# Softmax scores scaled and negated in place by the instruction that takes their minimum, the 1e-9 taken from padding columns, and new keys for the order of the work

## The chip, the core and the metric

The kernel runs on one core of a Trainium2 chip. The core's engines work side by side, each through its own queue in order: PE (TensorE, matrix products, with PEld its weight loads), DVE (VectorE), ACT (ScalarE), POOL (GpSimd) and SP (SyncE, which here only issues transfers). Matrix products write to PSUM; PSUM and SBUF are the two on-chip memories. The metric is the time on the device in microseconds (us); before the change it is 1153.44 us, the median of three runs between 1152.08 and 1154.72.

## What is computed

Attention with a threshold on the scores, and a feed-forward layer behind it:

```python
scores = scale * np.matmul(q, k.transpose(0, 1, 3, 2))          # q, k, v: (8, 8, 576, 64), scale = 1/8
thresh = np.max(scores, axis=-1, keepdims=True) - tau
scores = np.where(scores >= thresh, scores, -1000000000.0)
scores = scores - np.max(scores, axis=-1, keepdims=True)
attn = np.exp(scores)
attn = attn / (np.sum(attn, axis=-1, keepdims=True) + 1e-09)
x = np.matmul(attn, v)                                          # then laid out as (4608, 512)
h = x @ w_in                                                    # w_in: (512, 2048)
g = np.where(h >= 1, h, np.where(h <= -1, 0.0, (h + 1) ** 2 / 4))
out = g @ w_out                                                 # w_out: (2048, 512)
```

All of it is in float32 or wider. The kernel forms every product from float16 pairs, a high part and the rest, so each large product is a sum of several float16 products.

## The kernel before, in words

The attention part is cut into 288 score tiles of 128 query rows by 576 keys, for two heads at a time; 36 tiles belong to each of the 8 batches. One tile goes through this chain: `qk` (PE, L840) writes the scores into one of two PSUM buffers `s`; `smax` (DVE, L851 to L853) takes the negated row maximum and makes from it the bias of the exponential and the threshold; `sexp` (ACT, L856) writes the exponential of the scaled scores to SBUF (`e`); `smask` (DVE, L860) multiplies it by "score at or above the threshold" and sums the row; `sden` (DVE, L864 and L865) adds 1e-9 and takes the reciprocal; `snorm` (POOL, L868) multiplies the row; `shi` (ACT, L873) and `slo` (POOL, L876) make the float16 pair `hl`; `send` (SP, L879) transposes it by a transfer into `eT`; `av` (PE, L946) multiplies it with the values. Tiles 0 and 1 take a shorter way with a PE transpose (L912). The buffer `s` is free again when `smask` has read it.

The scale of a pair of heads is a column of the small tile `pc`, made on POOL by `scales3` (L391 to L394, four instructions for each of 32 pairs). It is one number for the exponential's scale and one for the threshold.

The feed-forward part follows by groups of 256 tokens: `ffn1` (PE, L1024) into one of three PSUM buffers `ph`, `relu` and `square` (ACT, L1030 and L1033), `gate` (DVE, L1037, in place in PSUM), the float16 pair by `ghi` (ACT, L1042) and `glo` (DVE, L1047), `ffn2` (PE, L1073) into the only PSUM buffer `acc`, and `evict` (ACT, L1093), which must have read `acc` before the next 128 tokens may begin there. In the first 200 us the weights are also unpacked (`b2`, `b3` on DVE, L660 and L664) and split (L725, L737), and PE fills long gaps with products of ones (`keep_warm`, L1109).

The order of the work on every engine is worked out ahead, in Python: each step is an `Op` with an engine, an assumed cost and a key, and a simulated list scheduler (`Plan.order`) takes, for each engine that falls idle, the ready step with the lowest key. The table `SHIFT` moves single keys. The order that comes out is fixed: each engine's queue on the chip holds the steps in it, and waits where a step's input is late. The assumed costs decide only the order.

Of the kernel before, what the change touches and what calls it, by code (L numbers as in the profile page):

```python
# [22 lines left out]
NPT = 2  # L23
# [26 lines left out]
WARM = (1.0, 200, 0.6, 0.056)  # L50

SHIFT = {
    "bits o": {7: -20, 8: -2, 12: -2},
    "den": {73: 5},
    "ffn": {8: 5, 12: -2, 19: 2, 21: -2, 22: -1.71, 23: -5},
    "ffn2": {1: 10, 9: -5, 10: 5, 16: 5, 18: -7.1, 19: -40, 23: -2, 24: 2, 25: -2, 26: -2},
    "load i": {0: -20, 1: -20, 11: -1.07},
    "load o": {8: 2},
    "load q k": {8: 4.48, 10: -4.1},
    "load v": {8: 19.78, 11: 5},  # L60
    "low o": {0: -19.88, 1: -18.87, 2: -16.6, 3: -10, 4: -10, 5: -5, 6: -5, 8: -2},
    "move": {8: -5, 9: -13.89},
    "norm": {39: -2, 58: -2, 69: -2},
    "parts o": {12: -2},
    "q k": {7: 20, 10: -5},
    "q k parts": {1: -8.79, 8: 5, 10: -5},
    "qk": {87: 25.43},
    "scale o": {0: -20},
    "send": {62: -5, 63: -10},
    "tile": {7: -2, 14: -2, 29: 5, 42: -2, 51: -2, 73: -10},  # L70
    "v": {1: 5, 2: 5},
    "v parts": {7: 17.66, 8: 35.35, 9: 33.43, 11: 11.83},
}
# [19 lines left out]
class Plan:  # L93
# [19 lines left out]

    def op(self, eng, cost, key, fn, after=(), take=(), uses=(), work=0.0, behind=None, mode=0, leave=0):

        o = Op(eng, cost, round(key, 3), fn, work)
        o.n = len(self.ops)
# [12 lines left out]
        return o  # L130
# [97 lines left out]
def attn_ffn_kernel(ctx: ExitStack, tc: tile.TileContext, qT, kT, vT, tau, w_in, w_out, out):  # L228
# [7 lines left out]
    B, H, D, S = qT.shape  # L236
# [8 lines left out]
    SP = -(-S // P) * P  # L245
# [36 lines left out]
    es = ring("e", 4, [SP], F32)  # L282
# [34 lines left out]
    def ap(b, arr):  # L317
        return arr[b.slot]
# [67 lines left out]
    def more_scales(cb, so, key):  # L386
        def scales3():
            c = ap(cb, pc)
            u = c[:, 8:14].rearrange("p (v t) -> p v t", t=2)
            x = c[:, 14:20].rearrange("p (v t) -> p v t", t=2)  # L390
            G.tensor_scalar(c[:, 24:27], u[:, :, 0], 2.0 ** 102 * D ** -0.5, 1.0, ALU.mult, ALU.mult)  # L391
            G.tensor_scalar(c[:, 27:30], x[:, :, 0], tcs[:, 2:3], 1.0, ALU.mult, ALU.mult)
            G.tensor_tensor(c[:, 24:27], c[:, 24:27], u[:, :, 1], ALU.mult)
            G.tensor_tensor(c[:, 27:30], c[:, 27:30], x[:, :, 1], ALU.mult)  # L394

        return plan.op("POOL", 0.85, key - 2, scales3, [so], uses=[cb])

    def add_qk(b, p, need):

# [408 lines left out]


    part_tr = {}  # L810
    eTb = {}
    av_op = {}
    prev = {}

    def chained(name, o):
        prev[name] = o
        return o

    def add_tile(j):
# [19 lines left out]
                        k = ap(kb, kk)[h, 0, kl, f * SH : (f + 1) * SH] if not b else ap(kb, kk)[:, hd, kl, f * SH : (f + 1) * SH]  # L839
                        T.matmul(ap(s, s_ps)[r, f, :SH], q, k, start=ql == kl == 0, stop=kl == 1)  # L840

        def sv():
            return ap(s, s_ps)[:, :, :SH]

        def halves(t):
            return t.rearrange("p (f n) -> p f n", f=2)

        def smax():

            t, c = ap(m, sm), ap(cb, pc)  # L850
            V.tensor_reduce(t[:, 0:1], sv(), AX.XY, ALU.max, negate=True)  # L851
            V.tensor_scalar(t[:, 1:2], t[:, 0:1], c[:, 24 + v : 25 + v], None, ALU.mult)  # L852
            V.tensor_scalar(t[:, 2:3], t[:, 0:1], -1.0, c[:, 27 + v : 28 + v], ALU.mult, ALU.add)  # L853

        def sexp():
            A.activation(halves(ap(e, es)[:, :S]), sv(), AF.Exp, bias=ap(m, sm)[:, 1:2], scale=ap(cb, pc)[:, 24 + v : 25 + v])  # L856

        def smask():
            t = ap(m, sm)
            V.scalar_tensor_tensor(halves(ap(e, es)[:, :S]), sv(), t[:, 2:3], halves(ap(e, es)[:, :S]), ALU.is_ge, ALU.mult, accum_out=t[:, 3:4])  # L860

        def sden():
            t = ap(m, sm)
            V.tensor_scalar(t[:, 4:5], t[:, 3:4], 1e-9, 1.0 / ESC, ALU.add, ALU.mult)  # L864
            V.reciprocal(t[:, 5:6], t[:, 4:5])  # L865

        def snorm():
            G.tensor_scalar(ap(e, es)[:, :S], ap(e, es)[:, :S], ap(m, sm)[:, 5:6], 1.0, ALU.mult, ALU.mult)  # L868

        w = S if b else SP  # L870

        def shi():
            A.activation(ap(x, hl)[:, :S], ap(e, es)[:, :S], AF.Copy)  # L873

        def slo():
            G.tensor_tensor(ap(x, hl)[:, w : w + S], ap(e, es)[:, :S], ap(x, hl)[:, :S], ALU.subtract)  # L876
# [6 lines left out]
        if b and v == 2 and i - 1 in av_op and tiles[first[i] - 1][1] == 2:  # L883
            o.behind.append(av_op[i - 1])
            av_op[i - 1].left += 1
        o = chained("max", plan.op("DVE", 1.03, jt, smax, [o, c2], take=[m], uses=[s, cb], behind=prev.get("max")))
        o = chained("exp", plan.op("ACT", 0.73, jt, sexp, [o], take=[e], uses=[s, m, cb], behind=prev.get("exp")))
        o = plan.op("DVE", 0.76, jt, smask, [o], uses=[s, m, e])
        o = plan.op("DVE", 0.28, plan.key("den", j, j), sden, [o], uses=[m])
        take = [eTb[i]] if j == first[i] else []  # L890
        if j >= NPT:
            o = chained("norm", plan.op("POOL", 0.73, jn, snorm, [o], uses=[e, m], behind=prev.get("norm")))
            o = chained("hi", plan.op("ACT", 0.58, jn, shi, [o], take=[x], uses=[e], behind=prev.get("hi")))
            o = plan.op("POOL", 1.26, jn, slo, [o], uses=[e, x])
            o = chained("tr", plan.op("SP", 1.45, plan.key("send", j, j), send, [o], take=take, uses=[x, eTb[i]], work=1.7, behind=prev.get("tr")))
# [266 lines left out]
```

## Time and profile before

| | before |
|---|---|
| median of 3 runs | 1153.44 us (1152.08 to 1154.72) |
| profiled execution, first to last instruction | 1151.1 us |
| PE busy | 1114.2 us (97%) |
| DVE busy | 949.8 us (83%) |
| ACT busy | 899.7 us (78%) |
| POOL busy | 800.9 us (70%) |
| mean granted TensorE clock | 0.991 |

The profile gives the span of one profiled execution; its own time has no other figure, and the median of the runs lies 2.3 us above that span. A busy share is a mean over the whole span, and the stretches differ: the start, with the weights, is not the middle. A row of a group gives line, engine, operation, what is written and read, the count, then busy time, the mean duration of one, and the idle time just before.

### The profile page before, as it was taken

The numbers are of one execution on the slowest core, as the hardware profiler recorded it, in microseconds if no ns is written. First come the engines' busy times: TensorE is split into PE (matmuls) and PEld (weight loads), VectorE is DVE, ScalarE is ACT, GpSimd is POOL, SyncE is SP. The second block draws the span as 40 slices with busy tenths as digits, with TensorE's granted clock in tenths as the row PEclk, the third lists the DMA queues.
The fourth block names the chain that finished last, engine by engine and source line by source line (L and its number), as shares of the span: only waits on it lengthen the run. The fifth ranks groups of instructions, "written<-read, shape, count | busy, mean of one in ns | idle before, by whom it ended". The sixth has DMA issues, their size and how long they took to land.

```text
span 1151.1 us, 27628 instructions
## 1 busy us (share of the span) xinstructions
PE 1114.2 (97%) x9627; PEld 770.1 (67%) x9627; DVE 949.8 (83%) x2995; ACT 899.7 (78%) x1692; POOL 800.9 (70%) x957
## 2 busy tenths in 40 slices
PE   8789999999999999999999999999999999999998
PEld 6447556767677577676677677676667677676673
DVE  5899987988889988899889989888889889885241
ACT  6989777979788789777887789776888788685362
POOL 4678999688875788668966887758966788654000
PEclk9969999999999999999999999999999999999999
DMA  8788699879895999777986899658876899554000
GB/s 322 289 220 151 124 196 203 165 135 206 163 181 98 187 167 200 148 127 168 202 182 109 154 207 204 121 108 186 182 178 103 157 183 171 103 103 83 19 1 28
DMA packets 435930, 179.41 MB, mean 156 GB/s; under 512 B 400464, under 2 KB 407632, under 8 KB 435792
## 3 DMA queue, kind: packets, MB, share of 16 engines
q1 hardware_dynamic: 435792, 177.67, 75.1%
q8 instruction: 75, 1.23, 0.4%
q14 instruction: 63, 0.52, 0.1%
HBM read 45.09 MB, written 9.44 MB: 47 GB/s over the span
## 4 chain that ended last, share of the span: by engine, by line
PE 63%; DVE 13%; POOL 8%; ACT 5%; issue 4%; DMA 4%; SPq 1%; ACTq 0%; DVEq 0%; POOLq 0%
PE ph L1024 24%; PE acc L1073 23%; PE s L840 8%; PE ph L946 7%; POOL hl L876 3%; DVE sm L851 3%; DVE e L860 3%; DMA eT<-hl 2%; POOL e L868 2%; POOL nat L461 1%; ACT e L856 1%; POOL raw L448 1%; DMA raw<-in_v_dram 1%; ACT hl L873 1%; DVE sm L852 1%
## 5 line engine op out<-in xcount | busy, mean ns | idle before, releaser
L876 POOL TENSOR_TENSOR hl<-e,hl 128x576 f16<-128x576 f32 x286 | 367.5, 1290 | 100.7 <-ACT hl L873 97.5
L1024 PE MATMUL ph<-x,WI 128*128 128x256 f16 (+1 forms) x4032 | 401.6, 257 | 1.1 <-DVE gb L1047 0.7
L1024 PEld LDWEIGHTS <-WI 128*128 128x128 f16 x4032 | 346.5, 98 | 52.9 <-issue 5.0
L868 POOL TENSOR_SCALAR e<-e,sm 128x576 f32<-128x576 f32 x286 | 218.4, 768 | 108.9 <-DVE sm L865 73.2
L856 ACT ACTIVATE e<-s,sm,pc 128x576 f32<-128x576 f32 x288 | 238.1, 832 | 53.3 <-DVE sm L852 37.9
L860 DVE SCALAR_TENSOR_TENSOR e<-s,sm,e 128x576 f32<-128x576 f32 x288 | 231.3, 812 | 30.5 <-ACT e L856 25.5
L873 ACT ACTIVATE hl<-e 128x576 f16<-128x576 f32 x286 | 194.9, 684 | 65.7 <-POOL e L868 53.1
L851 DVE TENSOR_REDUCE sm<-s 128x1 f32<-128x576 f32 x288 | 215.4, 748 | 25.8 <-PE s L840 24.0
L840 PE MATMUL s<-kk,qq 128*128 128x288 f16 (+3 forms) x1360 | 193.5, 290 | 15.1 <-DVE e L860 11.2
L1073 PE MATMUL acc<-WO,ga 128*128 128x512 f16 x864 | 206.5, 379 | 0.8 <-ACT ob L1093 0.8
L840 PEld LDWEIGHTS <-qq 128*128 128x128 f16 (+3 forms) x1360 | 113.3, 100 | 88.9 <-issue 45.3
L1037 DVE SCALAR_TENSOR_TENSOR ph<-ph,fcs,asq 128x512 f32<-128x512 f32 (+1 forms) x160 | 111.9, 700 | 51.8 <-ACT asq L1033 50.8
L1030 ACT ACTIVATE asq<-ph,fcs 128x512 f32<-128x512 f32 (+1 forms) x160 | 116.3, 738 | 48.6 <-PE ph L1024 47.9
L1073 PEld LDWEIGHTS <-ga 128*128 128x128 f16 x864 | 81.5, 98 | 82.7 <-issue 4.5
L946 PE MATMUL ph<-eT,vst 128*64 128x320 f16 (+2 forms) x1928 | 124.1, 280 | 3.7 <-DMA eT<-hl 1.3
L946 PEld LDWEIGHTS <-vst 128*64 128x64 f16 x1928 | 98.7, 110 | 26.7 <-issue 17.5
L1033 ACT ACTIVATE asq<-asq 128x512 f32<-128x512 f32 x144 | 90.9, 631 | 2.1
L1047 DVE SCALAR_TENSOR_TENSOR ga<-ph,fcs,ga 128x256 f16<-128x256 f32 (+1 forms) x160 | 70.6, 450 | 23.0 <-ACT WO L1042 8.8
L1042 ACT ACTIVATE ga<-ph,fcs 128x256 f16<-128x256 f32 (+1 forms) x160 | 70.3, 450 | 23.1 <-DVE ph L1037 20.8
L1073 PE MATMUL acc<-WO,gb 128*128 128x512 f16 x300 | 72.8, 379 | 0.0
L461 POOL TENSOR_TENSOR nat<-raw,nat 128x576 f16<-128x576 f32 x56 | 71.7, 1292 | 1.1 <-ACT nat L454 1.0
L852 DVE TENSOR_SCALAR sm<-sm,pc 128x1 f32<-128x1 f32 x288 | 61.7, 214 | 10.4
(167 smaller groups left out, 1245.8 us busy)
## 6 DMA issues: line engine op xcount, KB each, us to landing
kk<-nat SPq DMA_DIRECT2D x112, 144.0 KB, 2.7
raw<-in_v_dram SPq DMA_DIRECT2D x32, 288.0 KB, 3.9
raw<-in_q_dram SPq DMA_DIRECT2D x32, 288.0 KB, 4.1
raw<-in_k_dram SPq DMA_DIRECT2D x32, 288.0 KB, 3.8
WO<-in_moe_w_in_dram SPq DMA_DIRECT2D x16, 512.0 KB, 8.3
out_dram<-ob SPq DMA_DIRECT2D x32, 256.0 KB, 2.5
qq<-nat SPq DMA_DIRECT2D x112, 72.0 KB, 2.2
x<-in_moe_w_out_dram SPq DMA_DIRECT2D x10, 512.0 KB, 4.3
```

The source lines that it names most:

```text
L840: T.matmul(ap(s, s_ps)[r, f, :SH], q, k, start=ql == kl == 0, stop=kl == 1)
L851: V.tensor_reduce(t[:, 0:1], sv(), AX.XY, ALU.max, negate=True)
L856: A.activation(halves(ap(e, es)[:, :S]), sv(), AF.Exp, bias=ap(m, sm)[:, 1:2], scale=ap(cb, pc)[:, 24 + v : 25 + v])
L860: V.scalar_tensor_tensor(halves(ap(e, es)[:, :S]), sv(), t[:, 2:3], halves(ap(e, es)[:, :S]), ALU.is_ge, ALU.mult, accum_out=t[:, 3:4])
L868: G.tensor_scalar(ap(e, es)[:, :S], ap(e, es)[:, :S], ap(m, sm)[:, 5:6], 1.0, ALU.mult, ALU.mult)
L873: A.activation(ap(x, hl)[:, :S], ap(e, es)[:, :S], AF.Copy)
L876: G.tensor_tensor(ap(x, hl)[:, w : w + S], ap(e, es)[:, :S], ap(x, hl)[:, :S], ALU.subtract)
L946: T.matmul(o[hd * D : (hd + 1) * D, :n], vt[:, k, hd * D : (hd + 1) * D], t[:, kb, hd * n : (hd + 1) * n], start=m == 0, stop=m == len(blo ...
L1024: T.matmul(h[:, i], WTh["i"][:, u, wl * 512 + c * P : wl * 512 + (c + 1) * P], x[:, cc, xl, c0 : c0 + n].rearrange("p (t n) -> p t n", n=P ...
L1030: A.activation(tv()[:, :, c], hv()[:, :, c], AF.Relu, bias=fcs[:, b, q, 2 : 3], scale=fcs[:, b, q, 1 : 2])
L1037: V.scalar_tensor_tensor(hv()[:, :, c], hv()[:, :, c], fcs[:, b, q, 0 : 1], tv()[:, :, c], ALU.max, ALU.min)
L1073: T.matmul(ap(ab, accs), gv(h, gl)[:, x], WTh["o"][:, fc + i, wl * 512 : (wl + 1) * 512], start=fc + i == 0 and m == 0, stop=fc + i == NFC ...
```

## The change

`smax` becomes one `tensor_scalar` that multiplies the scores by a negative scale in place in PSUM and takes their minimum into `sm` by its accumulator. That minimum is the bias of the exponential, whose scale is now the constant -1. A new step `sthr` (DVE) adds tau for the threshold. `smask` compares with "at or below" and runs over one more column in each half, where `e` holds 0.5e-9 and `s` holds -3.0e38; both are written by `pads` (DVE) once for each buffer. So the row sum already holds the 1e-9, and `sden` is a reciprocal alone. `snorm` multiplies by the constant that `sden` had folded in. `scales3` makes one number instead of two, in two instructions. A second way through a tile (`mask_s`, `den_s`, `hi_s`, `lo_s`) is added but chosen for no tile, since `BYSUM` and `HOWS` are empty. The assumed costs of the steps change with this, a table `OFF` adds a constant to the keys of each kind of step, and `SHIFT` grows from 63 to 577 entries. Every matrix product stays as it was, but 188 products of ones are issued instead of 204.

```diff
 SHIFT = {
-    "den": {73: 5},
+    "_evict": {16: -56.49, 17: -0.75},
+    "den": {73: 5, 102: -1.12, 103: 30.8, 208: -2.8, 209: -250.25, 216: 8.96, 217: -8.51, 232: -45.33, 233: -10.82},
...
+OFF = {"av": -2.37, "b2": 28.6, "b3": 134.31, "consts": -11.77, "diff": 34.02, "ends_": -103.45, "evict": 96.25, "f0": -54.27, "f1": 0.14, "f2": 60.57, "f3": 110.84, "f4": 77.96, "f5": 14.45, "f_scale": -9.23, "ffn1": 0.16, "ffn2": 0.17, "fix": 55, "gate": -3.92, "ghi": -1.84, "glo": -1, "gram": 6.16, "hi": 3.9, "largest": -169.25, "lo": 0.04, "load": 0.21, "low": -19.44, "mixed": 325.86, "move": 1.36, "norm": 3.65, "o_scale": 23.37, "qk": -3.81, "relu": -87.18, "rest": -16.41, "rest1": -19.94, "scales": -1.36, "scales2": -6.69, "scales3": -0.38, "sden": -6.48, "send": -2.5, "sexp": 4.71, "shi": -4.76, "slo": -42.44, "smask": -1.99, "smax": 1.28, "snorm": -2.76, "split": -17.76, "split1": -11.94, "square": 0.81, "ssq": 166.71, "sthr": -4.13, "store": -6.38, "sums": 0.23, "tau_consts": 171, "thi": 193.92, "tlo": -9.03, "turn": -326.94, "warm_up": 249.88}
+BYSUM = set()
+HOWS = ""
+EPS = 1e-9
...
+        key = key + OFF.get(name, 0) + SHIFT.get("_" + name, {}).get(i, 0)
...
-        V.tensor_scalar(tcs[:, 2:3], tau_sb, 0.0, -(2.0 ** -102) * D ** 0.5, ALU.max, ALU.mult)
+        V.tensor_scalar(tcs[:, 2:3], tau_sb, 0.0, None, ALU.max)
...
-            x = c[:, 14:20].rearrange("p (v t) -> p v t", t=2)
-            G.tensor_scalar(c[:, 24:27], u[:, :, 0], 2.0 ** 102 * D ** -0.5, 1.0, ALU.mult, ALU.mult)
-            G.tensor_scalar(c[:, 27:30], x[:, :, 0], tcs[:, 2:3], 1.0, ALU.mult, ALU.mult)
+            G.tensor_scalar(c[:, 24:27], u[:, :, 0], -(2.0 ** 102) * D ** -0.5, 1.0, ALU.mult, ALU.mult)
             G.tensor_tensor(c[:, 24:27], c[:, 24:27], u[:, :, 1], ALU.mult)
-            G.tensor_tensor(c[:, 27:30], c[:, 27:30], x[:, :, 1], ALU.mult)
-
-        return plan.op("POOL", 0.85, key - 2, scales3, [so], uses=[cb])
+        return plan.op("POOL", 0.42, key - 2, scales3, [so], uses=[cb])
...
         def smax():
             t, c = ap(m, sm), ap(cb, pc)
-            V.tensor_reduce(t[:, 0:1], sv(), AX.XY, ALU.max, negate=True)
-            V.tensor_scalar(t[:, 1:2], t[:, 0:1], c[:, 24 + v : 25 + v], None, ALU.mult)
-            V.tensor_scalar(t[:, 2:3], t[:, 0:1], -1.0, c[:, 27 + v : 28 + v], ALU.mult, ALU.add)
+            V.tensor_scalar(sv(), sv(), c[:, 24 + v : 25 + v], None, ALU.mult, ALU.min, accum_out=t[:, 0:1])
+
+        def sthr():
+            t = ap(m, sm)
+            V.tensor_scalar(t[:, 2:3], t[:, 0:1], tcs[:, 2:3], None, ALU.add)
 
         def sexp():
-            A.activation(halves(ap(e, es)[:, :S]), sv(), AF.Exp, bias=ap(m, sm)[:, 1:2], scale=ap(cb, pc)[:, 24 + v : 25 + v])
+            A.activation(ev(), sv(), AF.Exp, bias=ap(m, sm)[:, 0:1], scale=-1.0)
+
+        def pads():
+            if e.slot not in padded["e"]:
+                padded["e"].add(e.slot)
+                V.memset(ap(e, es)[:, : 2 * (SH + 1)].rearrange("p (f n) -> p f n", f=2)[:, :, SH:], EPS / 2)
+            if s.slot not in padded["s"]:
+                padded["s"].add(s.slot)
+                V.memset(ap(s, s_ps)[:, :, SH : SH + 1], -3.0e38)
 
         def smask():
             t = ap(m, sm)
-            V.scalar_tensor_tensor(halves(ap(e, es)[:, :S]), sv(), t[:, 2:3], halves(ap(e, es)[:, :S]), ALU.is_ge, ALU.mult, accum_out=t[:, 3:4])
+            if early:
+                padded["s"].discard(s.slot)
+                padded["e"].discard(e.slot)
+                V.scalar_tensor_tensor(ev(), sv(), t[:, 2:3], ev(), ALU.is_le, ALU.mult, accum_out=t[:, 3:4])
+                return
+            pads()
+            V.scalar_tensor_tensor(ev(SH + 1), sv(SH + 1), t[:, 2:3], ev(SH + 1), ALU.is_le, ALU.mult, accum_out=t[:, 3:4])
 
         def sden():
             t = ap(m, sm)
-            V.tensor_scalar(t[:, 4:5], t[:, 3:4], 1e-9, 1.0 / ESC, ALU.add, ALU.mult)
-            V.reciprocal(t[:, 5:6], t[:, 4:5])
+            if early:
+                V.tensor_scalar(t[:, 3:4], t[:, 3:4], EPS, None, ALU.add)
+            V.reciprocal(t[:, 5:6], t[:, 3:4])
 
         def snorm():
-            G.tensor_scalar(ap(e, es)[:, :S], ap(e, es)[:, :S], ap(m, sm)[:, 5:6], 1.0, ALU.mult, ALU.mult)
+            G.tensor_scalar(ev(), ev(), ap(m, sm)[:, 5:6], ESC, ALU.mult, ALU.mult)
...
-        o = chained("max", plan.op("DVE", 1.03, jt, smax, [o, c2], take=[m], uses=[s, cb], behind=prev.get("max")))
-        o = chained("exp", plan.op("ACT", 0.73, jt, sexp, [o], take=[e], uses=[s, m, cb], behind=prev.get("exp")))
-        o = plan.op("DVE", 0.76, jt, smask, [o], uses=[s, m, e])
-        o = plan.op("DVE", 0.28, plan.key("den", j, j), sden, [o], uses=[m])
+        o = chained("max", plan.op("DVE", 0.78, jt, smax, [o, c2], take=[m], uses=[s, cb], behind=prev.get("max")))
+        o2 = plan.op("DVE", 0.18, jt, sthr, [o], uses=[m])
+        o = chained("exp", plan.op("ACT", 0.64, jt, sexp, [o], take=[e], uses=[s, m], behind=prev.get("exp")))
+        jd = plan.key("den", j, j)
...
```

Two places show what the new keys do to the queues. In an order row, a name ends in the buffer's number, and `x2` stands for two such instructions in a row.

The first place is DVE's queue at the start, where tiles 2 and 3 (statistics `sm_124` and `sm_125`, scores `s_61` and `s_62`) come, in the 20 to 75 us of the profile. Before:

```order
L851 TENSOR_REDUCE sm_124<-s_61 128x1
L852 TENSOR_SCALAR sm_124<-sm_124,pc_118 128x1
L853 TENSOR_SCALAR sm_124<-sm_124,pc_118 128x1
L851 TENSOR_REDUCE sm_125<-s_62 128x1
L852 TENSOR_SCALAR sm_125<-sm_125,pc_118 128x1
L853 TENSOR_SCALAR sm_125<-sm_125,pc_118 128x1
```

With the change:

```order
L908 TENSOR_SCALAR s_61,sm_124<-s_61,pc_118 128x2x288
L908 TENSOR_SCALAR s_62,sm_125<-s_62,pc_118 128x2x288
L912 TENSOR_SCALAR sm_124<-sm_124,tcs 128x1
L711 SCALAR_TENSOR_TENSOR WO<-x_106,ph_65 128x512
L912 TENSOR_SCALAR sm_125<-sm_125,tcs 128x1
L921 MEMSET e_93 128x2
L924 MEMSET s_61 128x2
L934 SCALAR_TENSOR_TENSOR e_93,sm_124<-s_61,sm_124,e_93 128x578
L921 MEMSET e_94 128x2
L924 MEMSET s_62 128x2
L934 SCALAR_TENSOR_TENSOR e_94,sm_125<-s_62,sm_125,e_94 128x578
```

Where three instructions of each tile stood, the two large ones now stand next to each other, the threshold of the first tile follows the second tile's minimum, a weight unpacking (L711, L660 before) stands between the two thresholds, and the four `MEMSET` rows are `pads`, which each buffer gets once.

The second place is the end of ACT's queue: the last steps of the feed-forward part, with the evictions of the last two blocks of 128 tokens (`ob`, L1093 before, L1201 now). Before:

```order
L1030 ACTIVATE asq_101<-ph_65,fcs 128x4x64 x2
L1033 ACTIVATE asq_101<-asq_101 128x512
L1042 ACTIVATE ga_111<-ph_65,fcs 128x2x64 x2
L1042 ACTIVATE WO<-ph_65,fcs 128x2x64 x2
L1093 ACTIVATE ob_102<-acc,scs 128x512
L1093 ACTIVATE ob_102<-acc,mix 128x512
```

With the change:

```order
L1150 ACTIVATE ga_110<-ph_64,fcs 128x2x64 x2
L1150 ACTIVATE gb_114<-ph_64,fcs 128x2x64 x2
L1201 ACTIVATE ob_102<-acc,scs 128x512
L1138 ACTIVATE asq_101<-ph_65,fcs 128x4x64 x2
L1141 ACTIVATE asq_101<-asq_101 128x512
L1150 ACTIVATE ga_111<-ph_65,fcs 128x2x64 x2
L1150 ACTIVATE WO<-ph_65,fcs 128x2x64 x2
L1201 ACTIVATE ob_102<-acc,mix 128x512
```

Before, the last two evictions stand together behind the last feed-forward step, and on PE the last 96 products of `ffn2`, 48 for each of the two blocks, follow each other with nothing between. Now the eviction of the block before the last stands ahead of that step, and PE has the step's 48 products of `ffn1` between the two blocks of `ffn2`.

More of the change, by code (lines that the diff above doesn't have):

```diff
@@ L810, in attn_ffn_kernel @@
     part_tr = {}
+    padded = {"e": set(), "s": set()}
     eTb = {}
@@ L894, in add_tile @@
[L894 to L895 removed]
+            ends = []
+            for how in HOWS or ("S" if j in BYSUM else "P"):
+                plan.alt = ("tile", j, how)
+                if how == "S":
+                    n = plan.op("DVE", 0.76, jt, mask_s, [o, o2], uses=[s, m, e])
+                    n = plan.op("DVE", 0.28, jd, den_s, [n], uses=[m])
+                    n = chained("hi", plan.op("ACT", 0.62, jn, hi_s, [n], take=[x], uses=[s, m], behind=prev.get("hi")))
+                    ends.append(plan.op("DVE", 0.74, jn, lo_s, [n], uses=[s, m, x]))
+                else:
+                    n = plan.op("DVE", 0.76, jt, smask, [o, o2], uses=[s, m, e])
+                    n = plan.op("DVE", 0.14, jd, sden, [n], uses=[m])
+                    n = chained("norm", plan.op("POOL", 0.73, jn, snorm, [n], uses=[e, m], behind=prev.get("norm")))
+                    n = chained("hi", plan.op("ACT", 0.58, jn, shi, [n], take=[x], uses=[e], behind=prev.get("hi")))
+                    ends.append(plan.op("POOL", 1.26, jn, slo, [n], uses=[e, x]))
```

80 lines of the change are left out of this document (51 added, 29 removed), and 43 rows, old and new, of the table SHIFT.

## The prediction, on record before the result

> **What bounds the kernel now.** The first view I read is the busy time of each engine in stretches (columns: stretch, its length, then busy us and instructions of PE, PEld, DVE, ACT and POOL, the granted clock, the DMA share and GB/s).
>
> ```profile
> span 1151.1 us, 27628 instructions
> 0.00:20.00 20.00, 15.93 (x139) 14.35 (x140) 7.82 (x21) 12.66 (x28) 6.79 (x36) 1.00 0.88 325
> 20.00:75.00 55.00, 42.84 (x331) 25.26 (x329) 49.19 (x161) 49.42 (x94) 35.04 (x58) 0.82 0.82 269
> 75.00:125.00 50.00, 47.10 (x599) 32.52 (x598) 47.55 (x164) 47.41 (x91) 42.82 (x51) 0.99 0.81 160
> 125.00:200.00 75.00, 71.34 (x645) 45.48 (x644) 64.71 (x199) 55.32 (x105) 73.23 (x87) 1.00 0.92 183
> 200.00:1100.00 900.00, 891.48 (x7544) 623.62 (x7542) 766.36 (x2417) 714.89 (x1335) 643.01 (x728) 1.00 0.77 151
> 1100.00:1152.00 52.00, 45.54 (x381) 28.90 (x378) 14.21 (x35) 20.03 (x44) 0.00 (x0) 0.99 0.05 16
> ```
>
> PE is the bound. From 200 to 1100 us it is busy 891.48 of 900 us, so the 900 us can give back 8.5 us at most, whatever the other engines save. From 20 to 200 us PE idles 55 + 50 + 75 - 42.84 - 47.10 - 71.34 = 18.7 us, and there other engines lead: DVE and ACT together up to 125 us (47.55 and 47.41 of 50), POOL after that (73.23 of 75). Saving on DVE is therefore worth nothing by itself; it is worth what PE waits for DVE.
>
> Next the waits of PE (engine and line, what it waited for, us in total, times, longest), first from 20 to 200 us, then from 200 to 1100 us:
>
> ```profile
> PE s L840 <- DVE e L860: 6.9, 7, 1.8
> PE ph L737 <- DVE wsc_i L326: 1.6, 1, 1.6
> PE acc L671 <- DVE WI L660: 1.4, 5, 0.5
> PE ph L946 <- DVE WI L660: 1.1, 1, 1.1
> PE s L840 <- DVE kk L459: 1.1, 2, 0.8
> ...
> PE s L840 <- DVE e L860: 4.3, 4, 2.2
> PE s L840 <- DVE sm L853: 1.3, 1, 1.3
> ```
>
> Most of it is `qk` waiting for a score buffer that `smask` (L860) has not read yet. In the first stretch the five waits shown for DVE make 12.1 us, in the second the two make 5.6 us. These 17.7 us are what a quicker DVE can reach directly.
>
> **The change on DVE.** The groups of one tile's statistics (the last with x46 for 20 to 200 us alone), the slowest DVE group on 576 elements, and the timeline of DVE (start, duration, operation) where two tiles follow each other in the middle:
>
> ```profile
> L851 DVE TENSOR_REDUCE sm<-s 128x1 f32<-128x576 f32 x288 | 215.4, 748 | 25.8 <-PE s L840 24.0
> L852 DVE TENSOR_SCALAR sm<-sm,pc 128x1 f32<-128x1 f32 x288 | 61.7, 214 | 10.4
> L853 DVE TENSOR_SCALAR sm<-sm,pc 128x1 f32<-128x1 f32 x288 | 58.8, 204 | 0.0
> L532 DVE SCALAR_TENSOR_TENSOR vb<-raw,scs,vb 128x576 f16<-128x576 f32 x28 | 35.2, 1257 | 0.3 <-POOL vb L527 0.2
> L851 DVE TENSOR_REDUCE sm<-s 128x1 f32<-128x576 f32 x46 | 34.3, 746 | 1.8 <-PE s L840 1.8
> ...
> 642.05 0.75 DVE L851 TENSOR_REDUCE sm<-s 128x1 f32<-128x576 f32 x1
> 642.83 0.21 DVE L852 TENSOR_SCALAR sm<-sm,pc 128x1 f32<-128x1 f32 x1
> 642.96 0.20 DVE L853 TENSOR_SCALAR sm<-sm,pc 128x1 f32<-128x1 f32 x1
> 643.08 0.75 DVE L851 TENSOR_REDUCE sm<-s 128x1 f32<-128x576 f32 x1
> ...
> 644.11 0.75 DVE L1037 SCALAR_TENSOR_TENSOR ph<-ph,fcs,asq 128x512 f32<-128x512 f32 x1
> 644.77 0.81 DVE L860 SCALAR_TENSOR_TENSOR e<-s,sm,e 128x576 f32<-128x576 f32 x1
> 645.50 0.08 DVE L860 DVE_READ_ACCUMULATOR e<-s,sm,e 128x1 f32 x1
> 645.50 0.81 DVE L860 SCALAR_TENSOR_TENSOR e<-s,sm,e 128x576 f32<-128x576 f32 x1
> ...
> 646.24 0.15 DVE L864 TENSOR_SCALAR sm<-sm 128x1 f32<-128x1 f32 x1
> 646.43 0.16 DVE L865 RECIPROCAL sm<-sm 128x1 f32<-128x1 f32 x1
> 646.51 0.13 DVE L864 TENSOR_SCALAR sm<-sm 128x1 f32<-128x1 f32 x1
> ```
>
> What counts in a full queue is the distance from one start to the next, not the duration. Before, the maximum takes 642.83 - 642.05 = 0.78 us, its two small steps 0.13 and 0.12 us, the 1e-9 and the reciprocal 646.51 - 646.24 = 0.27 us: 1.30 us a tile beside the mask.
>
> After, the new `smax` reads and writes 576 elements in PSUM and reads its accumulator out. The trace has no such instruction. Nearest are the mask, which reads PSUM and has an accumulator (645.50 - 644.77 = 0.73 us for 576 elements), and `gate`, which writes in place in PSUM (644.77 - 644.11 = 0.66 us for 512). Neither shows a price for writing in place or for the accumulator, so I take 0.73. The bounds are 0.66, from `gate`, and 1.26, the longest that DVE takes for 576 elements anywhere (L532). `sthr` is a step like L853, 0.12. The accumulator's read-out costs nothing where a step follows that does not need it (the second mask at 645.50 starts with it) and up to 0.08 where one does. The reciprocal alone is between 0.08 (646.51 - 646.43) and 0.16. That makes 0.73 + 0.12 + 0.04 + 0.12 = 1.01, a saving of 0.29 us a tile; with the two cheap ends 0.66 and 0.08 it is 0.44, with `smax` at 1.26 and the dear ends it is 1.62, a loss of 0.32. On 288 tiles, 0.29 is 84 us of DVE's 949.8. The wider mask (578 for 576) and the six fills of `pads` are below 2 us together, by the mask's own rate (0.73 us for 576) and L864's 0.15 for a tiny instruction.
>
> The tile's chain gets shorter as well. The exponential used to wait for the maximum and L852, 0.78 + 0.21 = 0.99 us; now it waits for `smax` and its read-out, 0.73 + 0.08 = 0.81.
>
> **On ACT and POOL.**
>
> ```profile
> L856 ACT ACTIVATE e<-s,sm,pc 128x576 f32<-128x576 f32 x288 | 238.1, 832 | 53.3 <-DVE sm L852 37.9 <-DVE sm L853 13.1 <-PE acc L1073 0.5
> L452 ACT ACTIVATE qq<-raw,pc 128x576 f16<-128x576 f32 x3 | 2.3, 773 | 0.0
> L454 ACT ACTIVATE nat<-raw 128x576 f16<-128x576 f32 x56 | 37.7, 685 | 12.1 <-POOL raw L448 11.4
> L392 POOL TENSOR_SCALAR pc<-pc,tcs 128x3 f32<-128x3 f32 x32 | 8.6, 270 | 2.9
> L394 POOL TENSOR_TENSOR pc<-pc 128x3 f32<-128x3 f32 x32 | 6.3, 197 | 0.0
> L868 POOL TENSOR_SCALAR e<-e,sm 128x576 f32<-128x576 f32 x286 | 218.4, 768 | 108.9 <-DVE sm L865 73.2 <-DVE sm L864 31.1 <-DVE ph L326 4.1
> ```
>
> The exponential loses its scale column and keeps its bias column. L452 and L454 differ by just such a column: 773 - 685 = 88 ns. So it saves between 0 and 0.088 us a tile; I take 0.088, 25 us over 288 tiles. POOL loses 270 + 197 ns for each of 32 pairs, 15 us. `snorm` works on two halves of 288 in place of one row; I cost it at the old 768 ns. Each of these is hidden by PE from 200 us on.
>
> **What reaches the end.** Three terms.
>
> Start, 20 to 200 us. L851 runs 46 times there, so DVE is relieved by 46 x 0.29 = 13 us, and ACT by 46 x 0.088 = 4 us. DVE's waits on the path are 12.1 us. But ACT is as full as DVE up to 125 us and POOL fuller after, and they are what is late next. I take half, 6 us; bounds 0 (ACT and POOL keep the pace) and 18.7 (PE never idle).
>
> Middle, 200 to 1100 us: 5.6 us wait for DVE there. Between 0 and PE's 8.5 I take 3, about half, since the tile's hold on the score buffer shrinks by 0.18 + 0.09 of 2.6 us (0.99, then 0.83 for the exponential and 0.81 for the mask, the products and handovers left out), so a late mask comes earlier but not always early enough.
>
> Tail. The timeline at the last block but one, PE's wait in brackets:
>
> ```profile
> 1135.06 0.69 ACT L1093 ACTIVATE ob<-acc,scs 128x512 f32<-128x512 f32 x1 [6.45 <-PE acc L1073]
> 1135.80 0.38 PE L1073 MATMUL acc<-WO,ga 128*128 128x512 f16 x1 [0.78 <-ACT ob L1093]
> ```
>
> The second block waits 0.78 us for the eviction. The new order puts 48 products of `ffn1` in between, which cover it: 0.8 us, all or nothing.
>
> The matrix products are the same, and the 16 products of ones less were fill for gaps: nothing. The sum is 6 + 3 + 0.8 = 9.8 us off the profiled span, 1151.1 - 9.8 = 1141.3 us. The median of the runs lies 2.3 us above the profiled span, so the forecast is **1143.6 us**.
>
> **The rivals.**
>
> *All of PE's idle time goes* (0.17). The keys are new for every kind of step, so steps can also be set so that what is late for other reasons comes in time. For it: only 28 us stand in the way (18.7 + 8.5 + 0.8). Against it: POOL's 73.23 of 75. With the lot gone it is 1153.4 - 28 = 1125.4; I put this case at 1131, four fifths of it.
>
> *Nothing comes through* (0.14). The gain is taken back by something that DVE does not set: 1153.4 us, or near. One such thing can be seen in the start:
>
> ```profile
> 55.00:75.00 20.00, 16.34 (x61) 7.66 (x62) 19.41 (x68) 17.17 (x32) 14.61 (x18) 0.50 0.86 234
> ```
>
> For 20 us PE had half its clock, though no wait of PE from 20 us on was longer than 2.2 us. A second such stretch in 75 to 200 us, where PE is 95% busy, would cost 20 x 0.5 x 0.95 = 9.5 us, the whole gain.
> The Trainium skill ("TensorE: Matmul & The Clock Gate", section "HAM oscillation — how this bites in real kernels") states it as an abstract rule that only idle gaps of PE of more than about 3.4 us bring the slow clock back. By that rule no such stretch should be here, and none would come; if the one that is here went too, the sum would fall by up to half of PE's 16.34 us, to some 1135 us, were PE and not DVE (19.41 of 20) the bound there. The trace does not agree with the rule, so I leave the clock as it is.
>
> *Slower: POOL's queue in the start* (0.21). From 125 to 200 us POOL has 1.8 us to spare in 75. Over the whole span its `snorm` waits for DVE's reciprocal like this:
>
> ```profile
> POOL e L868 <- DVE sm L865: 73.2, 72, 2.7
> ```
>
> That is 1.0 us each time, and nothing can pass it in the queue. If the new keys put some `snorm` there ahead of their reciprocals, each wait of 1 us moves POOL's whole remaining queue, with `hl`, the transfers and `av` behind it. PE has 75 - 71.34 = 3.7 us of its own in that stretch, and the rest of the gain is 3.8, so from 8 such waits on the change is slower. At 46 tiles in 180 us some 19 fall into the stretch; with 15 waits it is 1153.4 + 15 - 7.5 = 1161 us. For it: POOL's share, and a DVE order made for other costs than the chip's. Against it: DVE, which POOL waits for, does less.
>
> **How the numbers follow.** The forecast has 0.48, with its own range 1137 to 1150 (the start between 0 and 12). About 0.2% (2.3 us) is what a measurement of this kernel can tell from none. Faster: 0.48 + 0.17 - 0.01 = 0.64; within: 0.14; slower: 0.22. The range reaches into both outer cases, 1130 to 1160 us. It nearly holds the dear `smax` too: 46 x 0.32 = 15 us more on DVE in the start, half of it on the path, is 1153.4 + 7.5 = 1161 us, and the two nearest rows speak against it.
>
> **What would show it.** `smax` at 0.75 to 0.85 us in the groups, the exponential at 745, DVE busy near 865 us, POOL near 786. PE's waits for the mask (6.9 and 4.3) are halved, PE idles about 12 us from 20 to 200, and no wait for L1093's successor stands in the tail. I am wrong if `smax` exceeds 1 us, if POOL's waits for the reciprocal grow in 125 to 200 us, if a second stretch at half clock appears, or if PE's idle time from 200 to 1100 us rises above 8.5.

## The result, and the profile after

The changed kernel takes 1139.75 us, median of four runs (1138.46 to 1142.97); the kernel before, run beside it, 1154.08 us (1152.08 to 1154.95). The ratio is 0.9884, 95% interval 0.9867 to 0.9902: 13 to 14 us are gone where 9.8 were forecast. The profiled execution spans 1136.5 us, 14.6 less than before.

The stretches of the changed kernel, in the columns of the prediction's first view:

```profile
0.00:20.00 20.00, 14.43 (x140) 13.14 (x141) 7.46 (x21) 12.75 (x29) 6.86 (x36) 0.91 0.89 314
20.00:75.00 55.00, 43.23 (x363) 25.61 (x361) 50.88 (x169) 52.10 (x99) 35.58 (x53) 0.94 0.85 282
75.00:125.00 50.00, 43.50 (x606) 32.98 (x605) 45.77 (x152) 45.90 (x93) 43.58 (x50) 1.00 0.90 174
125.00:200.00 75.00, 72.32 (x618) 46.02 (x617) 64.69 (x183) 55.80 (x107) 69.63 (x78) 1.00 1.01 188
200.00:1100.00 900.00, 898.23 (x7640) 631.60 (x7638) 717.55 (x2170) 698.57 (x1341) 628.31 (x678) 1.00 0.77 149
1100.00:1152.00 52.00, 31.78 (x255) 18.60 (x252) 8.26 (x24) 11.37 (x28) 0.00 (x0) 0.97 0.05 16
```

Two readings tell where the time went. By idle time, the middle lost nearly all of it: PE idles 900 - 898.23 = 1.8 us there, where it idled 8.5. The start did not: 55 + 50 + 75 less PE's three busy times leaves 20.95 us from 20 to 200 us, where 18.7 stood. By finished work the start did gain. The whole of the first 200 us, before and then after:

```profile
0.00:200.00 200.00, 177.21 (x1707) 117.61 (x1708) 169.27 (x543) 164.80 (x315) 157.88 (x230) 0.95 0.86 215
0.00:200.00 200.00, 173.48 (x1721) 117.76 (x1722) 168.80 (x523) 166.54 (x324) 155.64 (x216) 0.97 0.93 223
```

The products of ones all fall there. Without them it is 1707 - 204 = 1503 products before and 1721 - 188 = 1533 after, so 30 more real products are done by 200 us, and in the middle 7640 - 7544 = 96 more. A product takes 900 / 7640 = 0.118 us on average there, so this is an estimate of 3.5 us for the start and 11.3 us for the middle. With the 0.8 us of the tail's wait that makes 15.6 us where the span lost 14.6. Products differ in length, so each estimate is good to a microsecond or two, no better.

How the middle can give back more than the 8.5 us that PE idled there, the largest group of products shows (`ffn1`, 200 to 1100 us, before and then after):

```profile
L1024 PE MATMUL ph<-x,WI 128*128 128x256 f16 (+1 forms) x3350 | 355.2, 263 | 0.7 <-DVE gb L1047 0.7
L1132 PE MATMUL ph<-x,WI 128*128 128x256 f16 (+1 forms) x3427 | 358.7, 263 | 0.0
```

A product's record lasts 263 ns, but each adds only 355.2 / 3350 = 0.106 us to PE's busy time, since the next one starts while the record still runs. A delay shorter than the rest of the record leaves no idle time. After the change 77 more products fit into 3.5 us more of busy time, 0.105 us each.

PE's waits of the changed kernel, from 20 to 200 us and then from 200 to 1100 us (what waited, for what; us, times, longest):

```profile
PE s L892 <- DVE e L934: 7.0, 7, 2.4
PE acc L722 <- DVE WO L711: 3.0, 3, 1.3
...
PE s L892 <- DVE e L934: 1.0, 2, 0.9
PE ph L1054 <- DVE WO L1155: 0.7, 1, 0.7
```

`qk` waits for a score buffer as long in the start as before (7.0 for 6.9 us), and hardly at all in the middle (1.0 for 4.3). The tail has no wait of PE left.

The groups of one tile's steps, and DVE's timeline where two tiles follow each other:

```profile
L908 DVE TENSOR_SCALAR_CACHE_REDUCE s<-s,pc 128x576 f32<-128x576 f32 x288 | 232.0, 820 | 63.2 <-PE s L892 62.7
L915 ACT ACTIVATE e<-s,sm 128x576 f32<-128x576 f32 x288 | 211.8, 742 | 72.8 <-DVE s L908 49.3 <-DVE sm L940 12.5 <-POOL hl L951 3.9
L943 POOL TENSOR_SCALAR e<-e,sm 128x576 f32<-128x576 f32 x286 | 220.4, 774 | 98.1 <-DVE sm L940 72.0 <-DVE sm L912 10.0 <-DVE scs L565 3.2
L912 DVE TENSOR_SCALAR sm<-sm,tcs 128x1 f32<-128x1 f32 x288 | 58.5, 208 | 1.9
L940 DVE RECIPROCAL sm<-sm 128x1 f32<-128x1 f32 x288 | 44.7, 158 | 4.6
L908 DVE DVE_READ_ACCUMULATOR s<-s,pc 128x1 f32 x288 | 40.8, 142 | 0.0
```

```profile
644.46 0.80 DVE L908 TENSOR_SCALAR_CACHE_REDUCE s<-s,pc 128x576 f32<-128x576 f32 x1
645.19 0.14 DVE L908 DVE_READ_ACCUMULATOR s<-s,pc 128x1 f32 x1
645.19 0.82 DVE L908 TENSOR_SCALAR_CACHE_REDUCE s<-s,pc 128x576 f32<-128x576 f32 x1
645.92 0.14 DVE L908 DVE_READ_ACCUMULATOR s<-s,pc 128x1 f32 x1
645.92 0.21 DVE L912 TENSOR_SCALAR sm<-sm,tcs 128x1 f32<-128x1 f32 x1
```

From start to start the new `smax` takes 645.19 - 644.46 = 0.73 us, the price taken in the prediction. Its record lasts 820 ns, longer than the old maximum's 748, so a reader who compares records alone sees a dearer instruction. What went is the second small step behind it, and at the reciprocal the 1e-9: DVE is busy 894.6 us for 949.8, ACT 876.5 for 899.7, POOL 784.0 for 800.9. PE's share is 97% in both kernels.

### The profile page after: what moved, and what is told of

Read it like the earlier page. It is cut to its first block, busy times and chain, and to the rows that moved or that the text cites. A ratio compares the mean times of both kernels' runs of the same rounds, so it can differ in the third digit from the quotient of the medians.

```text
span 1136.5 us, 27418 instructions
## 1 busy us (share of the span) xinstructions
PE 1103.5 (97%) x9611; PEld 768.0 (68%) x9611; DVE 894.6 (79%) x2715; ACT 876.5 (77%) x1692; POOL 784.0 (69%) x893
## 4 chain that ended last, share of the span: by engine, by line
PE 74%; POOL 3%; DVE 3%; ACT 2%; issue 2%; DMA 1%; SPq 0%; DVEq 0%; POOLq 0%; ACTq 0%
PE ph L1132 28%; PE acc L1181 28%; PE s L892 10%; PE ph L1054 8%; POOL e L943 1%; POOL hl L951 1%; DMA eT<-hl 1%; DVE s L908 1%; DVE e L934 1%; ACT hl L948 0%; POOL raw L499 0%; DVE vb L583 0%; ACT asq L1138 0%; POOL vb L578 0%; ACT e L915 0%
## 5 line engine op out<-in xcount | busy, mean ns | idle before, releaser
L908 DVE TENSOR_SCALAR_CACHE_REDUCE s<-s,pc 128x576 f32<-128x576 f32 x288 | 232.0, 820 | 63.2 <-PE s L892 62.7
L915 ACT ACTIVATE e<-s,sm 128x576 f32<-128x576 f32 x288 | 211.8, 742 | 72.8 <-DVE s L908 49.3
L934 DVE SCALAR_TENSOR_TENSOR e<-s,sm,e 128x578 f32<-128x578 f32 x286 | 230.9, 815 | 30.1 <-ACT e L915 26.6
L1181 PE MATMUL acc<-WO,ga 128*128 128x512 f16 x864 | 201.5, 379 | 0.0
L892 PE MATMUL s<-kk,qq 128*128 128x288 f16 (+3 forms) x1360 | 188.2, 287 | 10.7 <-DVE e L934 8.0
L1054 PEld LDWEIGHTS <-vst 128*64 128x64 f16 x1928 | 98.6, 110 | 25.9 <-issue 16.5
L1181 PE MATMUL acc<-WO,WI 128*128 128x512 f16 x288 | 67.2, 379 | 0.0
```

The source lines that it names most:

```text
L908: V.tensor_scalar(sv(), sv(), c[:, 24 + v : 25 + v], None, ALU.mult, ALU.min, accum_out=t[:, 0:1])
L915: A.activation(ev(), sv(), AF.Exp, bias=ap(m, sm)[:, 0:1], scale=-1.0)
L934: V.scalar_tensor_tensor(ev(SH + 1), sv(SH + 1), t[:, 2:3], ev(SH + 1), ALU.is_le, ALU.mult, accum_out=t[:, 3:4])
L1054: T.matmul(o[hd * D : (hd + 1) * D, :n], vt[:, k, hd * D : (hd + 1) * D], t[:, kb, hd * n : (hd + 1) * n], start=m == 0, stop=m == len(blo ...
L1181: T.matmul(ap(ab, accs), gv(h, gl)[:, x], WTh["o"][:, fc + i, wl * 512 : (wl + 1) * 512], start=fc + i == 0 and m == 0, stop=fc + i == NFC ...
```

## The experiments

Each ratio is to the kernel before, run beside it on the same chip, with the 95% interval. The theory was relief: PE waits for queues in which DVE's work stands, and less of that work lets the waits go. Its first rival was that the new keys make the gain.

**The new instructions in the old order, twice.** The old `SHIFT`, no `OFF`, the old assumed costs; the threshold's step is issued as a part of `smax`, right behind it. Every step stands where it stood before.

```diff
-    "_evict": {16: -56.49, 17: -0.75},
...
-    "den": {73: 5, 102: -1.12, 103: 30.8, 208: -2.8, 209: -250.25, 216: 8.96, 217: -8.51, 232: -45.33, 233: -10.82},
+    "den": {73: 5},
...
+OFF = {}
...
             V.tensor_scalar(sv(), sv(), c[:, 24 + v : 25 + v], None, ALU.mult, ALU.min, accum_out=t[:, 0:1])
+            V.tensor_scalar(t[:, 2:3], t[:, 0:1], tcs[:, 2:3], None, ALU.add)
```

> The instructions of the change in the order of the kernel before, step for step. Relief theory (the gain is less work on DVE and ACT and a shorter way from the scores to the mask): about 1143 us, most of the 14 us gained. Order theory (the gain is that the new keys put steps where PE does not wait for them): 1150 to 1154 us, PE's idle time from 200 to 1100 us still near 8 us. If both are needed: 1147 to 1150.

Measured: 1143.4 us, ratio 0.9924 (0.9901 to 0.9948). The second time, beside the changed kernel:

> The new instructions in the old order once more, beside the changed kernel. If the new keys are worth 3 to 4 us by themselves: 1142 to 1145 us, and a lower mean granted clock than the changed kernel's. If the earlier difference came from the chip or from chance: within 1 us of the changed kernel.

> The changed kernel as it is, beside the three that follow and on the same chip. 1138 to 1143 us.

Measured: 1145.58 us, ratio 0.9932 (0.9914 to 0.9951), and the changed kernel 1139.6 us, ratio 0.9888 (0.9863 to 0.9914). The first run meets the relief theory's 1143; the second lies 0.6 us above the 1142 to 1145 expected of it. So the instructions alone bring about 0.7%, two thirds or less of the gain, in an order made for the old ones. The rest comes with the order; which part of the order, the late threshold step below tells.

**The removed work put back into the new order.** Each kernel has the changed kernel's order step for step, and every added operation multiplies by one or passes its number on, so that only work is added: a small DVE step between the minimum and the exponential (A), one between the row sum and the reciprocal (B), a column in place of the exponential's constant scale (C), and two POOL instructions for each pair of heads in `scales3` (D).

```diff
             V.tensor_scalar(sv(), sv(), c[:, 24 + v : 25 + v], None, ALU.mult, ALU.min, accum_out=t[:, 0:1])
+            V.tensor_scalar(t[:, 1:2], t[:, 0:1], tcs[:, 4:5], None, ALU.mult)                      # A
...
-            A.activation(ev(), sv(), AF.Exp, bias=ap(m, sm)[:, 0:1], scale=-1.0)
+            A.activation(ev(), sv(), AF.Exp, bias=ap(m, sm)[:, 1:2], scale=tcs[:, 3:4])             # A, C
...
-            V.reciprocal(t[:, 5:6], t[:, 3:4])
+            V.tensor_scalar(t[:, 4:5], t[:, 3:4], 1.0, 1.0, ALU.mult, ALU.mult)                     # B
+            V.reciprocal(t[:, 5:6], t[:, 4:5])
...
+            G.tensor_scalar(c[:, 27:30], x[:, :, 0], tcs[:, 4:5], 1.0, ALU.mult, ALU.mult)          # D
+            G.tensor_tensor(c[:, 27:30], c[:, 27:30], x[:, :, 1], ALU.mult)                         # D
```

All four:

> The order of the changed kernel, with the work that it saved put back as idle steps: one small DVE step between the minimum and the exponential, one ahead of the reciprocal, a scale column for the exponential, two POOL instructions in scales3. Relief theory: about 1150 to 1154 us. Order theory: below 1143 us. If both are needed: 1143 to 1150.

A and B:

> The changed kernel with only the two small DVE steps of each tile put back. Relief theory, in which DVE carries it: 1147 to 1152 us. Order theory: within 2 us of the changed kernel's 1139.8. The busy time of DVE should rise by about 0.13 + 0.18 us a tile.

C alone:

> The changed kernel with only the scale column of the exponential put back: its mean should rise from 742 to about 830 ns. Relief theory: 1141 to 1144 us, ACT being as full as DVE up to 125 us. Order theory: within 1.5 us of 1139.8.

Measured: 1185.55 us with all (ratio 1.0292, 1.0272 to 1.0312), 1175.67 with A and B (1.0193, 1.0168 to 1.0218), 1144.81 with C alone (0.9935, 0.9917 to 0.9954). Each of the three lies above every range forecast for it. In the new order the two small DVE steps cost 36 us against the changed kernel, far more than the change gained. C costs 5 us for 22 us of ACT's time, though ACT is busy 79% at most. PE's waits for the mask in the middle with A and B, and that kernel's DVE timeline:

```profile
PE s L894 <- DVE e L937: 13.5, 22, 1.8
```

```profile
703.37 0.81 DVE L910 TENSOR_SCALAR_CACHE_REDUCE s<-s,pc 128x576 f32<-128x576 f32 x1
704.10 0.14 DVE L910 DVE_READ_ACCUMULATOR s<-s,pc 128x1 f32 x1
704.27 0.21 DVE L911 TENSOR_SCALAR sm<-sm,tcs 128x1 f32<-128x1 f32 x1
704.41 0.82 DVE L910 TENSOR_SCALAR_CACHE_REDUCE s<-s,pc 128x576 f32<-128x576 f32 x1
```

`qk` waits 13.5 us where 1.0 stood. And a small step that needs the accumulator costs more than its like elsewhere (0.12 us for L853 in the prediction's timeline): from minimum to minimum 704.41 - 703.37 = 1.04 us, 0.31 above the 0.73 of a minimum alone. The step starts 0.17 us behind the read-out's start, while in the changed kernel the next minimum, which does not need it, starts with it (645.19).

**Which of the two steps.** A lengthens the time for which a tile holds its score buffer, since the exponential waits for it; B does not, as the mask has read the buffer by then. If the buffer's hold is what PE waits for, A costs nearly all. If DVE's work is, both cost by their length.

> The changed kernel with one small DVE step between the minimum and the exponential. If the 36 us that two such steps cost come from the time a tile holds its score buffer: 1165 to 1175 us, nearly all of it. If they come from the work on DVE, whose two steps are of like size: about half, 1155 to 1160 us.

> The changed kernel with one small DVE step between the mask's sum and the reciprocal, so behind the point where the score buffer is free. Score buffer theory: 1141 to 1147 us. Work on DVE theory: about half of the 36 us, 1155 to 1160 us.

Measured: A alone 1153.08 us (ratio 1.0008, 0.999 to 1.0025), B alone 1148.03 us (0.9965, 0.995 to 0.998). DVE's busy time with A, then with B:

```profile
PE 1108.5 (96%) x9611; PEld 769.3 (67%) x9611; DVE 954.0 (83%) x3005; ACT 876.4 (76%) x1692; POOL 780.8 (68%) x893
```

```profile
PE 1108.9 (97%) x9611; PEld 771.2 (67%) x9611; DVE 929.7 (81%) x3005; ACT 874.8 (76%) x1692; POOL 780.9 (68%) x893
```

A adds 954.0 - 894.7 = 59.3 us and costs 1153.08 - 1139.6 = 13.5 us; B adds 35.0 and costs 8.4. That is 0.23 and 0.24 us per us of DVE's busy time. Busy time leaves out DVE's idle time where a small step has to wait for the one ahead of it (the last number; the step A, then the reciprocal behind B, which has 4.6 in the changed kernel):

```profile
L911 DVE TENSOR_SCALAR sm<-sm,tcs 128x1 f32<-128x1 f32 x288 | 61.7, 214 | 10.1
```

```profile
L943 DVE RECIPROCAL sm<-sm 128x1 f32<-128x1 f32 x288 | 47.3, 164 | 21.4
```

With it A takes 59.3 + 10.1 = 69.4 us of DVE's time and B 35.0 + 16.8 = 51.8, and the prices are 0.19 and 0.16. By either measure they are alike within the noise, 3 to 4 us on each cost, whether the buffer is held longer or not. Neither theory's sizes were met, but the buffer's hold as the one cause falls, since B's cost is clear of noise. Not separated is DVE's work from the way of a tile behind the mask, which both steps lengthen; but from 200 to 1100 us PE's waits with A, with B and with both have none for the transposed tile `eT`, and their largest item is the mask (5.1, 2.9 and 13.5 us). The two cost 21.9 us apart and 36 together, so the price rises with the load. And with A alone DVE has the load of the kernel before (949.8 us), while ACT and POOL keep their relief and the order is the new one: nothing of the gain is left.

**The threshold step out of the minimum's shadow.** In the kernel with the old order the threshold step stands right behind its minimum, as a dependent step. Here it is issued one DVE step later; all else stays in the old order.

```diff
+    waiting = []
...
         def smax():
...
-            V.tensor_scalar(t[:, 2:3], t[:, 0:1], tcs[:, 2:3], None, ALU.add)
+            flush()
+            waiting.append(t)
+
+        def flush():
+            for t in waiting:
+                V.tensor_scalar(t[:, 2:3], t[:, 0:1], tcs[:, 2:3], None, ALU.add)
+            waiting.clear()
...
         def smask():
...
+            flush()
```

> The new instructions in the old order, with the threshold's small step issued one DVE step later, so that it does not stand right behind the minimum that it needs. Every other step stays in the old order. If the time follows the busy time of DVE whatever the order: DVE from 916 to about 895 us, 1140 to 1142 us, as the changed kernel. If the new keys are worth 5 us by themselves: it stays at 1144 to 1146 us.

Measured: 1141.77 us, ratio 0.9906 (0.9891 to 0.992). The groups of the threshold step in the old order, right behind the minimum and then late (the last number is DVE's idle time ahead of it), then the late one's middle, and its one wait of PE in the tail:

```profile
L868 DVE TENSOR_SCALAR sm<-sm,tcs 128x1 f32<-128x1 f32 x288 | 61.7, 214 | 10.1
```

```profile
L874 DVE TENSOR_SCALAR sm<-sm,tcs 128x1 f32<-128x1 f32 x288 | 58.2, 209 | 0.3
```

```profile
200.00:1100.00 900.00, 898.59 (x7628) 629.82 (x7626) 715.04 (x2180) 700.33 (x1343) 632.45 (x679) 1.00 0.78 150
```

```profile
PE acc L1145 <- ACT ob L1165: 0.8, 1, 0.8
```

The middle is as full as in the changed kernel, with the 63 old entries in place of its 577. The kernel is 1.6 and 3.8 us faster than the two runs with the dependent step; their intervals overlap with its own, so the sign is likely and the size loose. What is left to the new keys is some 2 us, of which the tail's wait is 0.8; the intervals of this and the changed kernel overlap.

**Less of DVE's work still.** Two kernels in the new order. The first drops the threshold step; it leaves tau out of the computation, and the mask compares with the row's minimum itself.

```diff
-            V.tensor_scalar(t[:, 2:3], t[:, 0:1], tcs[:, 2:3], None, ALU.add)
+            pass
...
-            V.scalar_tensor_tensor(ev(SH + 1), sv(SH + 1), t[:, 2:3], ev(SH + 1), ALU.is_le, ALU.mult, accum_out=t[:, 3:4])
+            V.scalar_tensor_tensor(ev(SH + 1), sv(SH + 1), t[:, 0:1], ev(SH + 1), ALU.is_le, ALU.mult, accum_out=t[:, 3:4])
```

> The changed kernel without the threshold's small step: tau is left out and the mask keeps the row maximum alone, so its output is another. DVE falls by about 288 x 0.12 = 35 us. If the time goes on falling with DVE's work at the 0.23 us per us seen so far: 1131 to 1133 us. If what DVE can give is used up (PE idles 1 to 2 us from 200 to 1100 us already): 1137 to 1140 us, with the little that comes from the first 200 us.

The second moves one step of the values' float16 split from DVE to POOL:

```diff
-                V.scalar_tensor_tensor(t[:, 2 * S : 3 * S], ap(rb, raw), s[:, 2:3], t[:, :S], ALU.mult, ALU.subtract)
+                G.tensor_scalar(ap(rb, raw), ap(rb, raw), s[:, 2:3], 1.0, ALU.mult, ALU.mult)
+                G.tensor_tensor(t[:, 2 * S : 3 * S], ap(rb, raw), t[:, :S], ALU.subtract)
```

> The changed kernel with the rest part of the values (28 steps of about 1.5 us on DVE) made on POOL by two instructions at the same place in the program, 28 x 2.05 = 57 us more there. DVE falls by 40 us. If DVE's work alone sets the time: 1131 to 1138 us. If POOL, full from 125 to 200 us and waited for by ACT, is as close to the bound: 1142 us or slower.

Measured: 1140.3 us without the step (ratio 0.9895, 0.9879 to 0.991), 1152.38 us with the step on POOL (1.0003, 0.9989 to 1.0018). The middle without the threshold step, then 125 to 200 us and the middle with the values' step on POOL:

```profile
200.00:1100.00 900.00, 899.05 (x7651) 633.18 (x7649) 691.95 (x1937) 697.42 (x1342) 628.88 (x680) 1.00 0.78 150
```

```profile
125.00:200.00 75.00, 70.65 (x607) 44.44 (x603) 51.90 (x163) 50.68 (x97) 74.19 (x85) 1.00 0.93 173
200.00:1100.00 900.00, 889.61 (x7547) 624.92 (x7545) 693.90 (x2155) 693.69 (x1338) 673.31 (x731) 1.00 0.77 151
```

Another 32 us off DVE (863.0 busy) bring nothing: the middle has 1 us left to give, and by 200 us this kernel has finished 1686 - 188 = 1498 real products, fewer than the 1533 of the changed one, so the start does not follow DVE's load alone. And 33 us off DVE at the price of 45 on POOL (829.1 busy) lose the whole gain: POOL stands at 74.19 of 75 us in the start, and PE falls to 889.61 of 900 in the middle, where POOL is busy no more than 75%.

**The clock.** Between the old order with the late threshold step and the changed kernel another difference is seen: mean clock 0.986 to 0.991 against 0.994 to 0.997. The edit gives the former more products of ones, 312 for 204.

```diff
-WARM = (1.0, 200, 0.6, 0.056)
+WARM = (0.6, 200, 0.9, 0.056)
```

> The kernel with the new instructions in the old order and the late threshold step (1141.8 us) once more, with 312 products of ones in place of 204. Between it and the changed kernel (1139.7 us) some 2 us are left; its mean clock was 0.986 to 0.991, the changed kernel's 0.994 to 0.997, and its half-clock stretch lay at 52 to 80 us. Theory, the 2 us are that stretch: it shrinks, the mean clock comes to 0.993 or more, and the time to 1138 to 1140 us. Rival, TensorE is not what sets the pace there (DVE is busy 4.8 to 5 of each 5 us in that window), so that its clock costs nothing: 1141 to 1143 us at whatever clock, or more where the products of ones stand in the way.

Measured: 1141.43 us, ratio 0.9906 (0.9885 to 0.9928), mean clock 0.989 to 0.992. The window from 50 to 75 us of the kernel with 204, then with 312:

```profile
50.00:75.00 25.00, 20.45 (x84) 9.46 (x84) 22.81 (x78) 22.11 (x41) 19.20 (x23) 0.55 0.84 219
```

```profile
50.00:75.00 25.00, 20.84 (x114) 10.09 (x112) 22.98 (x78) 22.16 (x40) 19.43 (x23) 0.59 0.86 237
```

The stretch at half clock hardly moved, so this run doesn't settle what it costs. In the one execution profiled of each, 1859 - 312 = 1547 real products are done by 200 us where 1725 - 204 = 1521 were, and 7615 in the middle where 7628 were; the time is the same. Whether the last 2 us of the keys are the clock, the tail or the start stays open. The bulk of the gain is not the clock: the old order with the late step has most of it at a mean clock of 0.986 to 0.991, where the kernel before, beside it, has 0.984 to 0.991, and the kernel with the values' step on POOL has none of it at 0.989 to 0.996.

All runs in one table (DVE busy from each profile; time is the median):

| kernel | DVE busy, us | time, us | ratio |
|---|---|---|---|
| A, B, C, D back | 992.9 | 1185.55 | 1.0292 |
| A, B back | 990.0 | 1175.67 | 1.0193 |
| A back | 954.0 | 1153.08 | 1.0008 |
| before | 949.8 | 1154.08 | 1 |
| B back | 929.7 | 1148.03 | 0.9965 |
| new instructions, old order | 916.7 | 1145.58 | 0.9932 |
| C back | 899.2 | 1144.81 | 0.9935 |
| changed | 894.6 | 1139.75 | 0.9884 |
| old order, late threshold step | 887.8 | 1141.77 | 0.9906 |
| no threshold step | 863.0 | 1140.3 | 0.9895 |
| values' step on POOL | 861.2 | 1152.38 | 1.0003 |

With ACT and POOL as in the changed kernel, time follows DVE's busy time: by more than half a us per us above 954 us (1175.67 - 1153.08 over 990.0 - 954.0), by about 0.23 between 954 and 895, and not measurably below. These are a few points of this one kernel, not a law.

## Why the prediction was right, and where it was not

It was right in sign and in the main mechanism, DVE's relief shortening what PE waits for, and the time lies in the likeliest case's own range, 1137 to 1150. That the sum came as close as it did is in part luck: the middle gave some 8 us more than its term and the start 2.5 us less. Point by point:

- **The prices on the engines.** `smax` at 0.73 us from start to start, the exponential 742 ns for 745 expected, POOL 784.0 us for 786. DVE's busy time fell by 55 us, not 84, and the sign "near 865" was missed. The 84 were counted by distances between starts, which take in idle time ahead of dependent steps; busy time does not. That idle time fell too, from 10.4 at L852, 2.7 at L864 and 9.9 at L865 to 1.9 at L912 and 4.6 at L940, by 16.5 us. The rest of the difference was not traced.
- **Middle, 3 us (0 to 8.5): the term that failed.** The step was "I take 3, about half, since ... a late mask comes earlier but not always early enough", with PE's idle time as the bound. PE's visible idle time alone fell by 6.7 us, and the finished products say some 11. So the bound was too low too: busy time holds delays that the records cover, as the `ffn1` groups above show. The A and B runs show what the half was missing. The reason given, the tile's hold on its score buffer, is not the whole price, since B, which stands behind the hold, costs about as much per us of DVE's work as A: work on DVE delays the masks that come after it, wherever in a tile it stands. And the kernel with the late threshold step shows that nearly all of the middle is had by the relief, with none of the new keys and one step moved.
- **Start, 6 us (0 to 18.7).** 3.5 us by finished products, and not by the way forecast: PE idles more (20.95 for 18.7 us, 12 expected), and its waits for the mask are not halved (7.0 for 6.9). Fuller clock goes with it (0.94 for 0.82 from 20 to 75 us); that it is the cause was not shown. The 12.1 us of waits that the term was taken from left out those for ACT (WI, 1.4 and 1.1 us) and the smaller ones for DVE.
- **Tail, 0.8 us.** The wait is gone, as forecast.
- **"Nothing: fill for gaps", the products of ones.** That 16 fewer cost nothing was not tried by itself; 108 more in the old order left the time where it was.
- **The rivals.** *All of PE's idle time goes* was half right: the middle's went, the start's stayed. *POOL's queue in the start* did not come: `snorm` waits 72.0 us for the reciprocal over the whole span, 73.2 before, and POOL has 5.4 us to spare from 125 to 200 us, for 1.8. Its sign did show, too small to matter: in that stretch the changed kernel has two such waits, 1.3 us together, where before has none. That work on POOL can cost the gain, the kernel with the values' step on POOL shows, 12.6 us slower than the changed one; but it loses 93 products in the middle too, where POOL is not full, and `snorm` put ahead of its reciprocals was not tried. *Nothing comes through* by a second stretch at half clock: no long one came.

## What to carry to other kernels

A PE at 97% does not mean that the other engines' work is free: each queue in order holds steps for which PE waits a little, and the price per microsecond of their work (here some 0.2 of DVE's, none at a lighter load, more than twice that at a heavier one) is found by adding and removing work, not read from a busy share. Bound what such a stage can still give by its products per microsecond as well as by idle time, since records cover short delays. And where one instruction's accumulator feeds a small step, try another step between them: here that took DVE's idle time ahead of the step from 10.1 to 0.3 us and made the medians 1.6 and 3.8 us shorter.

## What the runs showed of the hardware that was not expected

- The in-place multiply with a minimum has its own name in the trace (TENSOR_SCALAR_CACHE_REDUCE), the pace of the mask (0.73 us for 576 elements), and a dearer read-out: 142 ns, where the mask's is 83.
- The half clock again came with no long wait. In the changed kernel it is shorter, as the window that the prediction showed at a clock of 0.50 now reads:

```profile
55.00:75.00 20.00, 16.79 (x122) 8.77 (x120) 19.75 (x60) 19.41 (x35) 17.24 (x21) 0.91 0.91 257
```

The longest wait of PE from 20 us on is 2.4 us, and the clock from 20 to 75 us is 0.94. The Trainium skill ("TensorE: Matmul & The Clock Gate", section "HAM oscillation — how this bites in real kernels") gives the abstract rule "no PE-idle gaps >~3.4µs". This trace keeps to it from 20 us on and still falls to half clock there, as that of before does, so here the rule was not enough to keep the full clock. What the clock is worth here stays open: PE finishes 122 products in the window where it finished 61, which are not all alike, while DVE is as full as before (19.75 of 20 us, 19.41 then).
